# Attention and gated MLP in one program: the first token block takes its weights from the decoder, and the planner's costs and order are redone

## The chip, the cores and the metric

The program runs on one core of a Trainium2 chip. The metric is the device time of one execution in microseconds (us); less is better. The engines are PE (matrix products, with PEld for its weight loads), DVE (vector), ACT (activation functions, copies with a scale), POOL (elementwise work) and SP, which here only issues DMAs, in the order in which the program lists them.

## What is computed

Inputs are q, k, v of shape (4, 8, 1152, 64) in float32, and three weight matrices of a gated MLP in float64. Each batch's attention is computed for query rows that are averaged in pairs, so 576 query rows meet 1152 keys; the 8 heads' results stand side by side as rows of 512, and the MLP is applied to these 2304 rows.

```python
q_pool = q.reshape(B, H, S // 2, 2, D).mean(axis=3)
scores = (1 / sqrt(D)) * q_pool @ k.T
attn = softmax(scores)                     # float32, over 1152 keys
x = (attn @ v) as rows of H * D            # 2304 x 512
g = x @ w_gate                             # 512 x 1536
out = (g * sigmoid(g) * (x @ w_val)) @ w_out   # 1536 x 512
```

## The kernel before, in words

**Precision.** PE multiplies in a reduced float32 form (F32R). Each float32 operand is therefore split in a high part (a cast) and a low part (the rest), and a product is made of two or three matmuls.

**Attention.** The work is cut in 16 pairs of heads, `p`, each with nine tiles of 128 query rows; a *tile* below is one of these 144. A tile (`s_tile`) makes scores in three pieces of 384 keys: one in a PSUM bank `sb`, two in the double bank `sa` (PE, L499). DVE takes a running minimum of the first piece (L505) and then of the other two (L507, once per tile, so L507 counts tiles), ACT makes the exponentials `pn` (L515). A `unit` transposes three tiles' exponentials for 128 keys into a bank `pt` (PE, L557), ACT casts the high part `ph` (L562), DVE subtracts the low part `pl` (L565), PE multiplies both with `vs` into `po` (L573). `evac` adds the results up (L607, L610). POOL sums the denominators (L620, L621), DVE inverts them (L624), SP writes them to DRAM (`rs<-rc`, L632), reads them back spread over partitions (`rb<-rs`, L637), POOL multiplies (L644) and SP stores the result (`xd<-xf`, L646). For each pair q, k, v are loaded (L356 to L365), split on POOL, transposed on PE (L453) and copied to `kt`, `qt`, `qrt` by ACT or DVE (L458, L460).

**Weights.** The MLP's weights are 36 blocks of 512 KB: for each of 12 feature groups `f` a gate, a value and an output block. `decode_w(n)` turns a float64 block into the two float32 parts by integer work: SP loads the words `wraw` (L278, L280; two buffers), ACT takes the size (L286), DVE clamps, shifts, adds the low bits and the sign (L289, L293, L297, L301), ACT casts the high part into a buffer `ws` (L307), POOL subtracts the low part (L310), SP stores both to a DRAM block `wd` (L313). There is one `ws` buffer: the next block's cast waits until the store of this one has landed. The 36 decodes are placed from tile 27 to tile 70 (`DEC0`, `DEC1`).

**MLP.** Three blocks of 512 tokens run between the attention tiles from tile 39 on, the first 512 tokens (block 0) about from tile 39 to 75, blocks 1 and 2 each 36 tiles later; the last 768 tokens run as a `tail` with nothing beside them. For each `f`, `fetch` reads gate and value weights from `wd` into `wg` (3 buffers) and the output weight into `wo` (3 buffers) (L792); `hidden` makes the two first products (L801) in banks `pg`, the gate on ACT and DVE (L814 to L843), and the split `hh`, `hl` (L847, L851); `out_tile` multiplies with `wo` (L907) for three `f` at a time, and the results are added on DVE (L943). Before block 0 begins, the two `pg` banks are lent to the attention of the first batch (pairs 0 to 3): `other` gives every second `sb` and every third `pt` the name `pg`, and both uses take the two banks in turn.

**The order.** Every step is an `op` with a cost in us on its engine, a position in tiles, the steps that must precede it, the buffers that it takes and gives back, and `more`, the time from its end until its result is there (for a DMA, the landing). `Plan.order` builds a schedule from these costs, and the instructions of every engine are issued in that order; nothing is decided when the program runs, and each engine executes its list strictly in order. Where a step may run on one of several engines, the schedule picks one, or `KEPT` fixes it. `SHIFTS` is a table of two characters for each step that moves the step's position, by up to about five tiles; "PP" is zero. The planner's costs for DVE are lower than the trace's durations in many lines (0.468 us for L565, whose mean is 551 ns); the DMAs' `more` is between 1.6 and 3.5 us.

Of the kernel before, what the change touches and what calls it, by code (L numbers as in the profile page):

```python
# [20 lines left out]
def f32_of_bits(bits):  # L21
# [14 lines left out]
        "PPPPPPPiPPPPPPPPMSPPPPPPPPPPPPPPPPPPPPPPPPPPPPB8PPPPPPPPPPPPPPPPPPPPPPPPPPPPPPPPPPPPPPPPPPPPPPPPPPPPPPPP"  # L36
        "PPPPPPPPP\\PPPPPPPPPPPPPPPPPPPPPPPPPPPPPPP'PPPPPPPPPPPPPPPPPPPPPPPPPPPPPPPPQHPPPPPPPPPPPOPPPPPPPPPPPPPPNS"
        "PPPPPPPPPPPPPPPPPPPPPPPPPPPPPPPPPPPPR?PPPPPPPPPPS#PPPPPPPPPPPPLMPPPPPPPPPPPPOtPPPPPPPPPPPPPPPPPPPPPPPPPP"
        "PPPPPPPPPPPPPPPPPPPPPPQlPPPPPPPPPPPPPPPPPPPPPPPPPPPPPPPPPPPPPPPeT/PPPPPPPPPPPPPPPPPqPPPPPPPPPPPPPPPPPPPP"
        "PPPPPPPPPPPPPPPPPPPPPPPPPPL1PPTWPPPPPPPPPPPPPPPPPPPPPPPPPPPPPP"  # L40
    ),
    "pair": (
        "R%PPPPPPPPPPPPPPPPPPPPPPPPPPPPPPPPPPPPPPPPPPPPPPPPPPPPPPPPPPPPPPPPPPPPPPPPPPPPPPPPPPPPPPPPPPPPPPPPPPPPPP"
        "PPPPPPPPPPPPPPPPPPPPPPPPPPPPPPPPPPPPPPPPPPPPPPPrPPPPPPPPPPPPPPPPPPPPPPPPPPPPPPPPPPPPPPPCPPPPPPPPPPPPP0PP"
        "PPPPPPPPPPPPPPPPPPPPPPPPPPPPPPPPPPPPPPPPPPPPPPPPPPPPPPPPPPPPNnPPPPPPPPPPPPPPPPPiPPPPPPPPPPPPPPPPPPPPPPPP"
        "PPPPPPPPOOPPPPPPPPPPPPPPPPQ?PPPPPPPPPPPPPPPPPPPPPPPPPPPPPPQ?PPPPPPPPPPPPPPPPPPPPPPPPPPPPPPPPPPPPPPPPPPPP"
        "PPPPPPPPPPPPPPPPPPPPPPPPPPPPPPPPPPPP"
    ),
# [986 lines left out]
```

## Time and profile before

| | us |
|---|---|
| three runs | 1139.1, 1142.38, 1141.29 (median 1141.29) |
| the profiled execution | 1147.5, of which its span (first to last instruction) is 1145.7 |
| PE busy | 1031.4 (90% of the span) |
| DVE busy | 759.3 (66%) |
| ACT busy | 631.1 (55%) |
| POOL busy | 337.2 (29%) |
| mean granted PE clock | 0.954 |

In the profile, a row of the slices gives the busy share of 40 equal slices of the span in tenths; each slice is 28.6 us. A row of the waits reads: engine, the tile and line that waited, what released it, and us in total, times, longest. In a row of the timeline stand start, length, engine, line and operation, and in brackets the idle time ahead of it and who ended it. "SPq" is SP's issuing of a DMA.

### The profile page before, as it was taken

How to read it: one execution, taken by the hardware profiler on the slowest of the kernel's cores; microseconds unless marked ns; L12 is line 12 of the kernel's file. 1: busy time of each engine (PE TensorE's matmuls, PEld its weight loads, DVE VectorE, ACT ScalarE, POOL GpSimd, SP SyncE). 2: the span in 40 equal slices, each digit the busy share in tenths (PEclk: the TensorE clock that was granted, in tenths of full speed). 3: DMA queues.
4: the chain of work that ended last, by engine and by line, in shares of the span. 5: the costliest groups of instructions: out<-in, count | busy, mean ns of one | idle time of the engine just before them, and what ended most of it. 6: DMA issues, size and time to landing. Idle time of an engine off the chain costs nothing.

```text
span 1145.7 us, 17106 instructions
## 1 busy us (share of the span) xinstructions
PE 1031.4 (90%) x5937; PEld 918.2 (80%) x5937; DVE 759.3 (66%) x1427; ACT 631.1 (55%) x1471; POOL 337.2 (29%) x316
## 2 busy tenths in 40 slices
PE   5988877687878879999998999999999997899997
PEld 4878866576767767888997989889889986799996
DVE  5777777796878969868665767667676763422222
ACT  4776765476556655765664565657575753111112
POOL 5043142543526235252413232334141101200000
PEclk8999988788998989999998999999999998999999
DMA  4233366867697786565545464564443625634432
GB/s 154 63 82 77 61 197 176 262 232 161 225 209 229 251 186 207 161 204 176 146 107 136 153 119 154 119 202 115 125 117 94 113 88 90 225 116 127 140 114 74
DMA packets 94390, 171.46 MB, mean 150 GB/s; under 512 B 27424, under 2 KB 46752, under 8 KB 94304
## 3 DMA queue, kind: packets, MB, share of 16 engines
q1 hardware_dynamic: 94128, 169.98, 53.7%
q8 instruction: 47, 0.77, 0.3%
q14 instruction: 39, 0.32, 0.1%
q0 software_dynamic: 96, 0.26, 0.1%
q10 hardware_dynamic: 80, 0.13, 0.0%
HBM read 132.12 MB, written 28.39 MB: 140 GB/s over the span
## 4 chain that ended last, share of the span: by engine, by line
PE 67%; DMA 13%; DVE 10%; ACT 5%; issue 3%; SPq 1%; POOL 1%; DVEq 0%; POOLq 0%; ACTq 0%
PE pg L801 23%; PE po L573 10%; PE sa L499 8%; PE pt L557 8%; PE pg L907 6%; DMA wd<-ws 4%; PE sb L499 4%; DMA wg<-wd 3%; DMA rs<-rc 3%; PE pt L453 2%; ACT pn L515 2%; DVE junk L507 2%; DVE pl L565 2%; PE sa L907 1%; PE pt L907 1%
## 5 line engine op out<-in xcount | busy, mean ns | idle before, releaser
L801 PE MATMUL pg<-x,wg 128*128 128x512 f32 (+1 forms) x1152 | 320.4, 394 | 14.2 <-DMA wg<-wd 10.8
L565 DVE TENSOR_TENSOR pl<-pt,ph 128x384 fp32r<-128x384 f32 x396 | 213.1, 551 | 109.8 <-ACT ph L562 107.0
L562 ACT CAST ph<-pt 128x384 fp32r<-128x384 f32 x396 | 182.6, 483 | 141.4 <-PE pt L557 127.4
L801 PEld LDWEIGHTS pg<-x,wg 128*128 128x128 f32 x1152 | 206.1, 193 | 37.2 <-DMA wg<-wd 11.9
L557 PE MATMUL pt<-ident,pn 128*128 128x128 f32 x1056 | 188.4, 285 | 19.5 <-DVE pl L565 9.1
L573 PE MATMUL po<-ph,vs 128*128 128x384 f32 (+1 forms) x576 | 175.5, 318 | 1.7 <-DVE xs L610 1.7
L573 PE MATMUL po<-pl,vs 128*128 128x384 f32 (+1 forms) x576 | 172.2, 313 | 4.4 <-DVE pl L565 4.0
L507 DVE TENSOR_SCALAR_CACHE_REDUCE junk<-sa,mx 128x768 bf16<-128x768 f32 x144 | 145.8, 1012 | 42.4 <-PE sa L499 40.9
L557 PEld LDWEIGHTS pt<-ident,pn 128*128 128x128 f32 x1056 | 138.9, 147 | 38.8 <-issue 7.1
L515 ACT ACTIVATE pn<-sa,mx 128x768 f32<-128x768 f32 x144 | 130.9, 909 | 61.4 <-DVE junk L507 61.1
L499 PE MATMUL sa<-kt,qt 128*128 128x384 f32 x512 | 145.8, 371 | 6.9 <-ACT pn L515 6.8
L573 PEld LDWEIGHTS po<-pl,vs 128*128 128x128 f32 x576 | 111.7, 194 | 14.8 <-DVE pl L565 7.0
L573 PEld LDWEIGHTS po<-ph,vs 128*128 128x128 f32 x576 | 111.6, 194 | 11.1 <-DVE xs L610 1.7
L907 PE MATMUL pg<-wo,hh 128*128 128x512 f32 x288 | 114.7, 403 | 1.0 <-ACT hh L847 0.6
L499 PEld LDWEIGHTS sa<-kt,qt 128*128 128x128 f32 x512 | 91.5, 201 | 16.5 <-ACT pn L515 9.5
L851 POOL TENSOR_TENSOR hl<-ta,hh 128x512 fp32r<-128x512 f32 x36 | 47.2, 1310 | 161.9 <-ACT hh L847 141.8
L843 DVE TENSOR_TENSOR ta<-pg,ta 128x384 f32<-128x384 f32 x48 | 26.8, 558 | 94.8 <-ACT ta L839 67.6
L505 DVE TENSOR_REDUCE mx<-sb 128x1 f32<-128x384 f32 x128 | 70.6, 551 | 28.3 <-PE sb L499 27.1
L310 POOL TENSOR_TENSOR ws<-w,ws 128x512 fp32r<-128x512 f32 x36 | 49.3, 1368 | 121.3 <-ACT ws L307 107.0
L499 PE MATMUL sb<-kt,qt 128*128 128x384 f32 x224 | 65.3, 374 | 21.1 <-ACT pn L515 21.0
L847 ACT CAST hh<-ta 128x512 fp32r<-128x512 f32 (+1 forms) x60 | 34.7, 579 | 83.0 <-DVE ta L843 54.3
L515 ACT ACTIVATE pn<-sb,mx 128x384 f32<-128x384 f32 x128 | 75.8, 592 | 0.1
(116 smaller groups left out, 1635.2 us busy)
## 6 DMA issues: line engine op xcount, KB each, us to landing
wg<-wd SPq DMA_DIRECT2D x96, 512.0 KB
wo<-wd SPq DMA_DIRECT2D x48, 512.0 KB
wd<-ws SPq DMA_DIRECT2D x36, 512.0 KB
vraw<-in_v_dram SPq DMA_DIRECT2D x16, 576.0 KB
kraw<-in_k_dram SPq DMA_DIRECT2D x15, 576.0 KB
qraw<-in_q_dram SPq DMA_DIRECT2D x15, 512.0 KB
qt<-qt SPq DMA_DIRECT2D x60, 128.0 KB
wraw<-in_moe_w_gate_dram SPq DMA_DIRECT2D x12, 512.0 KB
```

Source lines behind the costliest of these rows:

```text
L310: nc.gpsimd.tensor_sub(cell["s"][:, 1], cell["w"], cell["s"][:, 0])
L499: nc.tensor.matmul(o[:, 0:KW], lhsT=lhsT, rhs=s[f"kt{jj}"][:, n * KW:(n + 1) * KW], start=(m == 0), stop=(m == len(terms) - 1))
L505: nc.vector.tensor_reduce(mx[:, 0:1], cell["b"][:, 0:KW], axis=AX.X, op=ALU.min)
L507: nc.vector.tensor_scalar(junk, cell["a"][:, :, 0:KW], mx[:, 0:1], None, op0=ALU.min, op1=ALU.min, accum_out=mx[:, 1:2])
L515: nc.scalar.activation(o[:, 0:2 * KW].rearrange("p (a k) -> p a k", a=2) if n == 0 else o[:, 2 * KW:S], cell["a"][:, :, 0:KW] if n == 0 el ...
L557: nc.tensor.transpose(cell["ps"][:, o:o + P], src, ident)
L562: nc.scalar.copy(cell["h"], cell["ps"][:, 0:GW])
L565: nc.vector.tensor_sub(cell["l"], cell["ps"][:, 0:GW], cell["h"])
L573: nc.tensor.matmul(o[:, c0:c1], lhsT=s["vs"][:, j, c, :], rhs=cell[x][:, c0:c1], start=(c == 0 and n == 0 and x == "h"), stop=(c == KC - 1 ...
L801: nc.tensor.matmul(o, lhsT=w[:, a, c * P:(c + 1) * P], rhs=x[c][b][:, 0:n], start=(c == 0 and m == 0), stop=(c == NC - 1 and m == 2))
L851: (nc.gpsimd if eng == "Pool" else nc.vector).tensor_sub(cell["l"][:, 0:n], cell["a"][:, 0:n], cell["h"][:, 0:n])
L907: nc.tensor.matmul(o, lhsT=cell[a][:, t * P:(t + 1) * P], rhs=w[:, b, :], start=(first and m == 0), stop=(last and m == 2),)
```

## The change

It touches the weights of block 0, the lent banks and the planner.

- **Block 0 uses decoded weights in place.** `decode` takes a `wg` or `wo` buffer instead of `ws` and leaves the two parts there; block 0's products read them from it. The store to `wd` stays, for blocks 1, 2 and the tail, but the cast no longer waits for the one before: it waits for a free `wg` or `wo` buffer, which is free when block 0's products and the store have both read it. Block 0's 36 fetches from `wd` are gone. `ws` is gone, and `wg` has four buffers instead of three.
- **The decodes move.** They are placed at block 0's own steps, five, four and one tiles ahead of the product (`DECODE`), instead of evenly from tile 27 to 70.
- **Banks.** `pg` becomes two names: `pg0` is lent to `sb`, `pg1` to `pt`, also for the first tiles of pair 4; in the MLP the gate product is always in `pg0` and the value product in `pg1`, output tiles alternate.
- **The planner** gets higher DMA costs, a new rule for the order in which takers of a buffer stand (`turn`: by the position of the step that begins the chain), and new tables `SHIFTS` and `KEPT`: most steps now have a shift, and some steps a fixed engine.

```diff
 SHIFTS = {
     "pair": (
-        "R%PPPPPPPPPPPPPPPPPPPPPPPPPPPPPPPPPPPPPPPPPPPPPPPPPPPPPPPPPPPPPPPPPPPPPPPPPPPPPPPPPPPPPPPPPPPPPPPPPPPPPP"
+        "lxIUO%I4<PN`TQK>_,=3=zUU@XX$PYWoPP0P>@q\\1OoZqP9KRP>YZOoP:O_[OPV\\;S/PYX3>CMvLkIVGWFcI_T7IGPwOrP_N`FvP'N7"
...
 KEPT = {
     "pair": (
-        "........."
+        "AAD.D.AA."
...
-    def op(self, cost, pos, fn, after=(), take=(), give=(), more=0.0, load=0):
+    def op(self, cost, pos, fn, after=(), take=(), give=(), more=0.0, load=0, turn=None):
...
         for name in take:
-            self.takers[name].append((pos, n))
+            self.takers[name].append((pos if turn is None else self.ops[turn][1], n))
...
         def hi():
-            cell["s"] = stage.tile([P, 2, 512], F32R, name="ws", tag="ws", bufs=decoding["ws"])
-            nc.scalar.copy(cell["s"][:, 0], cell["w"])
+            cell["w"] = new(("wg", "wg", "wo")[i], [P, 2, 512], F32R)
+            nc.scalar.copy(cell["w"][:, 0], cell["f"])
...
         def put():
-            nc.sync.dma_start(out=wd[n], in_=cell["s"].bitcast(F32))
+            nc.sync.dma_start(out=wd[n], in_=cell["w"].bitcast(F32))
...
-    decoding = {"wraw": 2, "wa": 1, "w32": 1, "ws": 1}
+    decoding = {"wraw": 2, "wa": 1, "w32": 1}
...
-            "wg": 3, "wo": 3, "hh": 3, "hl": 3, "ta": 2, "tb": 2, **{f"ob{t}": 1 for t in range(TB // P)},
+            "wg": 4, "wo": 3, "hh": 3, "hl": 3, "ta": 2, "tb": 2, **{f"ob{t}": 1 for t in range(TB // P)},
...
-        banks = {"sa": 1, "sb": 1, "pt": 2, "po": 1, "pg": 2}
+        banks = {"sa": 1, "sb": 1, "pt": 2, "po": 1, "pg0": 1, "pg1": 1}
...
-        def other(tag, p, turn):
+        def other(tag, p, turn, early):
-            return "pg" if p < HP and turn else tag
+            return {"sb": "pg0", "pt": "pg1"}[tag] if turn and (p < HP or p == HP and early) else tag
...
-            y = op({"SP": 1.7}, z + 8 - LEAD + 1.7, lambda p=p: spread(p, 0), after=[y], give=("rc",), more=2.1)
-            y = op({"SP": 1.3}, z + 8 - LEAD + 1.8, lambda p=p: spread(p, 1), after=[y], take=("rb",), more=2.1)
+            y = op({"SP": 1.7}, z + 8 - LEAD + 1.7, lambda p=p: spread(p, 0), after=[y], give=("rc",), more=10.0)
+            y = op({"SP": 1.3}, z + 8 - LEAD + 1.8, lambda p=p: spread(p, 1), after=[y], take=("rb",), more=4.0)
...
-        DEC0, DEC1 = 27.0, 70.0
-        for n in range(3 * NF):
-            plan.part("decode")
-            load, size, clamp, shift, low, sign, hi, lo, put = decode_w(n)
-            pos = DEC0 + (DEC1 - DEC0) * n / (3 * NF)
-            x = op({"SP": 1.46}, pos - 1.0, load, take=("wraw",), more=2.1, after=[at_tile(pos)])
+        def decode(n, tag, pos):
+            cell, load, size, clamp, shift, low, sign, hi, lo, put = decode_w(n)
+            x = f = op({"SP": 1.6}, pos - 1.0, load, take=("wraw",), after=[at_tile(pos - 1.0 + LEAD)], more=4.0)
...
-            x = op({"ACT": 0.53}, pos + 0.06, hi, after=[x], take=("ws",))
+            x = op({"ACT": 0.53}, pos + 0.06, hi, after=[x], take=(tag,), turn=f)
             x = op({"Pool": 1.5}, pos + 0.07, lo, after=[x], give=("w32",))
-            wput[n] = op({"SP": 0.8}, pos + 0.08, put, after=[x], more=3.0, give=("ws",))
+            wput[n] = op({"SP": 1.6}, pos + 0.5, put, after=[x], more=4.0)
+            return x, cell
...
-            return op({"SP": 0.8}, pos, load, after=[wput[n]], take=(tag,), more=3.5), cell
+            return op({"SP": 1.6}, pos, load, after=[wput[n]], take=(tag,), more=3.8), cell
...
         def block(blk, s0):
+            decoded = []
+            if blk == 0:
+                plan.part("decode")
+                for f in range(NF):
+                    at = s0 + 9.0 * (f // FG) + 2.0 * (f % FG)
+                    decoded.append([decode(3 * f + i, ("wg", "wg", "wo")[i], at + DECODE[i]) for i in range(3)])
...
-                    wg = [fetch(3 * f + i, "wg", pos - 3.0 + i) for i in range(2)]
-                    wo.append(fetch(3 * f + 2, "wo", pos + 1.0))
+                    if blk == 0:
+                        *wg, w = decoded[f]
+                        wo.append(w)
+                    else:
+                        wg = [fetch(3 * f + i, "wg", pos - 3.0 + i) for i in range(2)]
+                        wo.append(fetch(3 * f + 2, "wo", pos + 1.0))
...
+        DECODE = (-5.0, -4.0, -1.0)
```

How the instructions move. In the rows below, a row is one instruction of an engine in the order of its list: the line, the operation, the tile written and read, its shape, and a count where equal rows follow each other. The changed kernel's line numbers are 6 higher in these places.

First place: ACT in the middle of the decode, about tile 54, before. `wa` is the decoder's working tile, `ws` the decoded parts, `kt` the keys of the next pair, `ph` the high parts of the exponentials, `pn` the exponentials:

```order
L286 ACTIVATE wa<-wraw 128x512
L607 COPY tmp<-po 64x192
L562 CAST ph<-pt 128x384
L307 CAST ws<-w_3884 128x512
L458 ACTIVATE kt_3862<-pt 128x512
L562 CAST ph<-pt 128x384
L607 COPY tmp<-po 64x192
```

ACT with the change, where it copies the keys of the same pair:

```order
L313 CAST wo<-w_3739 128x512
L568 CAST ph<-pt 128x384
L292 ACTIVATE wa<-wraw 128x512
L464 ACTIVATE kt_3796<-pt 128x512
L568 CAST ph<-pt 128x384
```

The decoder's cast still stands a step or two ahead of the copy of the keys, but it writes a buffer of `wo` instead of the one `ws`.

Second place: SP around the eleventh and twelfth decoded block, before. `wd` is a DRAM block, `rs`, `rb`, `rc` the denominators' path:

```order
L313 DMA wd_87<-ws 128x1024
L278 DMA wraw<-in_moe_w_val_dram 128x4x128
L792 DMA wg<-wd_84 128x1024
L632 DMA rs_65<-rc 128x4x1 x2
L633 DMA rs_65<-rc 2x64x1
L313 DMA wd_88<-ws 128x1024
L280 DMA wraw<-in_moe_w_out_dram 128x512
L637 DMA rb<-rs_65 64x576 x2
L792 DMA wg<-wd_86 128x1024
```

SP with the change, at the store of the same two blocks:

```order
L319 DMA wd_86<-wg 128x1024
L366 DMA qraw<-in_q_dram 128x2x512
L371 DMA qraw<-in_q_dram 64x128 x2
L284 DMA wraw<-in_moe_w_val_dram 128x4x128
L319 DMA wd_87<-wg 128x1024
L652 DMA xd_58<-xf 128x576
```

The stores read `wg`, and no fetch `wg<-wd` stands between them.

Third place: SP where the last pair of heads ends, before. The `wg` rows fetch for block 2 and then for the tail:

```order
L633 DMA rs_76<-rc 2x64x1
L792 DMA wg<-wd_108 128x1024
L637 DMA rb<-rs_76 64x576 x2
L792 DMA wg<-wd_110 128x1024
L792 DMA wg<-wd_111 128x1024
L792 DMA wg<-wd_77 128x1024
```

SP with the change, at the same place:

```order
L639 DMA rs_76<-rc 2x64x1
L798 DMA wg<-wd_108 128x1024
L798 DMA wg<-wd_111 128x1024
L643 DMA rb<-rs_76 64x576 x2
L798 DMA wg<-wd_77 128x1024
L798 DMA wg<-wd_78 128x1024
```

Two fetches for block 2 now stand ahead of `rb<-rs`, which waits for `rs` to land; a third, `wd_110`, has moved further ahead, out of the rows shown.

More of the change, by code (lines that the diff above doesn't have):

```diff
@@ L529, in s_tile @@
             done["s", p, i] = a
-            x = op({"ACT": 0.88}, pos + EXP_AT, lambda: exp(0), after=[x], take=("pn", "sums") if i == 0 else ("pn",), give=("sa",))
+            x = op({"ACT": 0.88}, pos + EXP_AT, lambda: exp(0), after=[x], take=("pn", "sums") if i == 0 else ("pn",), give=("sa",), turn=f)
             done["p", p, i] = op({"ACT": 0.56}, pos + EXP_AT + 0.01, lambda: exp(1), after=[x], give=(sbank, "mx"))
@@ L578, in unit @@
             a = op({"PE": 0.33}, pos, tr, after=[done["p", p, i] for i, _ in tiles], take=(tbank,), load=-1)
-            b = op({"ACT": 0.37}, pos + HI_AT, hi, after=[a], take=("ph",))
+            b = op({"ACT": 0.37}, pos + HI_AT, hi, after=[a], take=("ph",), turn=a)
             x = op({"DVE": 0.468}, pos + LO_AT, lo, after=[b], give=(tbank,))
@@ L859, in hidden @@
                         {"PE": 3 * n * 0.000452}, pos + i * GV + c * GV / NC, lambda i=i, c=c: product(i, c),
-                        after=[x_done[key][c], wg[i][0], y, *([] if late is None else [at_tile(pos + i + LEAD - late)])],
-                        take=("pg",) if c == 0 else (), load=1, give=(give[i] if last else ()),
+                        after=[x_done[key][c], wg[i][0], y, *(put[i:i + 1] if last else ()), *([] if late is None else [at_tile(pos + i + LEAD - late)])],
+                        take=(f"pg{i}",) if c == 0 else (), load=1, give=(give[i] if last else ()),
                     )
@@ L890, in load @@
                 load_x(key, g0, n)
-            a = op({"SP": 2.4}, pos, load, after=[done["x", p] for p in pairs], take=take, more=2.5)
+            a = op({"SP": 3.2}, pos, load, after=[done["x", p] for p in pairs], take=take, more=4.0)
             cost = {"Pool": 0.3 + n * 0.0033, "DVE": 0.14 + n * 0.0016}
@@ L946, in out_tile @@
             for m in range(FG):
-                y = op({"PE": 0.69}, pos + 0.25 * m, lambda m=m: product(m), after=[hs[m][0], wo[m][0], y, at_tile(pos + LEAD - LATE)], take=("pg",) if m == 0 else (), load=1)
+                y = op({"PE": 0.69}, pos + 0.25 * m, lambda m=m: product(m), after=[hs[m][0], wo[m][0], y, at_tile(pos + LEAD - LATE)], take=(pg,) if m == 0 else (), load=1)
             if g == 0:
-                z = op({"ACT": 0.48, "DVE": 0.6}, pos + 0.8, put, after=[y], take=(f"ob{t}",), give=("pg",))
+                z = op({"ACT": 0.48, "DVE": 0.6}, pos + 0.8, put, after=[y], take=(f"ob{t}",), give=(pg,))
             else:
-                z = op({"DVE": 0.6}, pos + 0.8, put, after=[y, obs["w", t]], give=("pg",))
+                z = op({"DVE": 0.6}, pos + 0.8, put, after=[y, obs["w", t]], give=(pg,))
             obs["w", t] = z
```

199 lines of the change are left out of this document (103 added, 96 removed).

## The prediction

> **What bounds the kernel now.** First the page's slices, to see which engine is full where, and what the clock and the DMAs do meanwhile.
>
> ```profile
> PE   5988877687878879999998999999999997899997
> DVE  5777777796878969868665767667676763422222
> PEclk8999988788998989999998999999999998999999
> DMA  4233366867697786565545464564443625634432
> ```
>
> From the 16th slice on PE is full but for a dent at slice 34. Before that it is not, least of all in slices 5 to 15, where DVE and the DMAs are busiest. Next I counted the tiles by L507, which runs once per tile, in four windows, and asked for the engines' busy time in the same windows.
>
> ```profile
> L507 DVE TENSOR_SCALAR_CACHE_REDUCE junk<-sa,mx x24: 1006/1017/1020, 27.3 to 128.0; 128x768 bf16<-128x768 f32 x24
> L507 DVE TENSOR_SCALAR_CACHE_REDUCE junk<-sa,mx x12: 1002/1016/1019, 133.6 to 202.7; 128x768 bf16<-128x768 f32 x12
> L507 DVE TENSOR_SCALAR_CACHE_REDUCE junk<-sa,mx x37: 1000/1008/1019, 214.1 to 500.9; 128x768 bf16<-128x768 f32 x37
> 27.00:134.00 107.00, 96.13 (x652) 88.39 (x652) 80.51 (x167) 77.71 (x194) 31.18 (x33) 0.97 0.30 77
> 134.00:214.00 80.00, 56.41 (x318) 49.09 (x315) 58.69 (x116) 48.35 (x115) 28.78 (x27) 0.86 0.62 170
> 214.00:507.00 293.00, 251.19 (x1384) 217.64 (x1385) 240.37 (x425) 183.24 (x415) 124.93 (x103) 0.91 0.73 213
> 507.00:941.00 434.00, 426.29 (x2571) 381.73 (x2570) 303.50 (x584) 267.21 (x638) 124.65 (x121) 0.99 0.51 132
> 941.00:1000.00 59.00, 48.86 (x234) 40.72 (x233) 25.23 (x43) 17.48 (x35) 11.01 (x12) 0.94 0.61 156
> ```
>
> The windows' columns are window, length, busy PE, PEld, DVE, ACT, POOL, granted clock, DMA share, GB/s. I call the middle ones stages 1 to 4. Plain attention takes 107 / 24 = 4.46 us per tile. Stage 1 (tiles 28 to 39, decoding begins) takes 80 us for 12, which is 6.7 each. Stage 2 (tiles 40 to 76, decoding and block 0) takes 293 for 37. Stage 3 has the same MLP work per tile, from weights in DRAM, and PE is 426.29 / 434 = 0.98 busy: there is nothing to win but 7.7 us. PE's idle time is 23.6 us in stage 1, 41.8 in stage 2, 10.1 in stage 4. So the decoding is where the time lies, and the waits of stage 2 say why (the last row is of the whole span).
>
> ```profile
> ACT ws L307 <- DMA wd<-ws: 27.4, 7, 9.6
> PE pt L453 <- ACT kt L458: 16.2, 2, 9.0
> PE sb L499 <- ACT pn L515: 12.7, 5, 7.0
> ACT ws L307 <- DMA wd<-ws: 36.8, 11, 9.6
> ```
>
> One such wait in the timeline, SP's, ACT's and PE's rows:
>
> ```profile
> 330.48 2.18 SPq L313 DMA_DIRECT2D wd<-ws  x1
> 344.21 0.62 ACT L307 CAST ws<-w 128x512 fp32r<-128x512 f32 x1 [9.62 <-DMA wd<-ws]
> 344.74 0.59 ACT L458 ACTIVATE kt<-pt 128x512 fp32r<-128x512 f32 x1
> 345.38 0.37 PE L453 MATMUL pt<-identr,ks 128*128 128x128 f32 x1 [8.98 <-ACT kt L458]
> ```
>
> The cast of a decoded block needs the one `ws`, whose store was issued 13.7 us earlier. ACT stands still for 9.62 us, the copy of the next keys stands behind the cast, and PE waits 8.98 us for that copy. DVE and POOL stop too.
>
> **Stage 1.** Of the 36 decodes, these rows of L289 put 8 in stage 1 and 28 in stage 2.
>
> ```profile
> L289 DVE TENSOR_SCALAR wa<-wa x8: 408/422/1098, 149.4 to 211.3; 128x512 f32<-128x512 f32 x8
> L289 DVE TENSOR_SCALAR wa<-wa x28: 406/424/1483, 220.4 to 471.7; 128x512 f32<-128x512 f32 x28
> L289 DVE TENSOR_SCALAR wa<-wa 128x512 f32<-128x512 f32 x36 | 20.5, 568 | 2.1 <-ACT wa L286 1.8
> L293 DVE TENSOR_SCALAR wa<-wa 128x512 int32<-128x512 int32 x36 | 24.6, 683 | 0.4
> L297 DVE SCALAR_TENSOR_TENSOR wa<-wraw,wa 128x512 int32<-128x512 int32 x36 | 35.5, 987 | 0.3
> L301 DVE SCALAR_TENSOR_TENSOR w<-wraw,wa 128x512 int32<-128x512 int32 x36 | 32.0, 890 | 6.0 <-POOL ws L310 5.4
> ```
>
> In DVE's list of the changed kernel one decode stands ahead of the 40th tile, 35 behind. Stage 1 becomes plain attention: 12 x 4.46 = 53.5, and one decode on DVE, 0.568 + 0.683 + 0.987 + 0.890 = 3.13 us: 57 in all, a gain of **23**. It cannot be much more, as PE has 96.13 / 2 = 48 us of work in 12 such tiles. It is 17 if ACT again stands 6.6 us at the first raw block:
>
> ```profile
> ACT wa L286 <- DMA wraw<-in_moe_w_gate_dram: 9.6, 2, 6.6
> ```
>
> **Stage 2.** *Gone:* the waits for the store, 27.4 us, with PE's 16.2 + 12.7 = 28.9 behind ACT; I take 27.4 off the path. 293 - 27.4 = 265.6. *Added:* 35 - 28 = 7 decodes, 7 x 3.13 = 21.9 us on DVE, which then has 240.4 + 21.9 = 262.3 us of work. That does not fit unseen in 265.6. Its share today is 240.4 / 293 = 0.82; 0.98 is what the planner reaches for PE in stage 3. I take 0.93, nearer to the upper end, since the stops that kept DVE idle are those that go: 262.3 / 0.93 = 282, a gain of **11**. Bounds: 0.98 gives 268 (gain 25), 0.88 gives 298 (loss 5).
>
> The 36 fetches for block 0 (18.9 of the 293 x 0.213 = 62 MB that stage 2 moved) cost PE nothing by themselves; without them the remaining transfers have more room. I count no gain for that, nor for a better clock than 0.91. What the change puts in the way: the cast now waits for a `wg` or `wo` buffer, with the exponentials and casts of attention queued behind it on ACT, and PE behind those. With four `wg` the buffer's last reader stands a tile or more earlier in PE's list, and its store several tiles earlier, so I take nothing; if that cover fails it costs at most what the old wait did, 27.4. And block 0's products wait for POOL's low part itself, with attention's matmuls behind them on PE. In the changed lists most casts stand two to five tiles ahead of their first product, a few only one. The nearest row of PE waiting for weights is below: 3.6 us each, so four of them would cost 14. I take nothing, as a decoded part is there without a landing.
>
> ```profile
> PE pg L801 <- DMA wg<-wd: 10.8, 3, 5.7
> ```
>
> The skill has a price for a store that speaks against this term. The Trainium skill, "DMA: Bandwidth & Descriptors", section "Anatomy of one DMA", fits about 2.0 us plus bytes / 436e3 (for DMAs issued from GpSimd): an estimate of 3.2 us for 512 KB. By that the store would have landed before ACT came to the cast, the 27.4 would be nothing to win, and the sum would end at 1125 instead of 1098. The trace shows 13.7 us from issue to cast, and decides.
>
> **Stage 3 and 4: fetches ahead of a blocked queue.** At the end of a pair SP waits for `rs` to land, and fetches stand behind it.
>
> ```profile
> 943.15 0.55 SPq L633 DMA_DIRECT2D rs<-rc  x1
> 943.84 3.51 SPq L792 DMA_DIRECT2D wg<-wd  x1
> 955.63 1.12 SPq L637 DMA_DIRECT2D rb<-rs  x2
> 956.84 15.17 SPq L792 DMA_DIRECT2D wg<-wd  x4
> 959.99 1.65 PE L801 MATMUL pg<-x,wg 128*128 128x512 f32 x3 [5.74 <-DMA wg<-wd]
> PE pg L801 <- DMA wg<-wd: 5.0, 2, 4.8
> ```
>
> PE ran dry for 5.74 us here, and for 5.0 in stage 3 (last row). The planner's 2.1 us for this landing becomes 10.0, and in the new SP list two fetches of block 2 stand ahead of `rb<-rs` here, a third earlier still. I take **5.5** in stage 4 and **4** in stage 3; both could be nothing. All of stage 3 is in a new order, though: it can gain at most its 7.7 us of idle time, and lose about as much (+8) where new orders meet real durations.
>
> **Start and banks.** Up to 134 us the bank names and the order change. Before stage 1 PE idles 107 - 96.1 = 10.9 us; two uses that share two banks in turn wait for each other, and no longer do. Between a gain of 5 and a loss of 4 I take 0. In the MLP gate and value alternated anyway: 0. The tail behind 1000 us is PE's own work: 0.
>
> **Sum.** -23 - 11 - 4 - 5.5 = -43.5. The profiled execution took 1147.5 (span 1145.7); it lies 6.2 above the median of the runs, 1141.3. 1147.5 - 43.5 = 1104, and on the runs' scale **1098 us**.
>
> **Rivals.** All on the runs' scale.
>
> *DVE stays the limit (faster, by less).* For it: 35 decodes in 37 tiles, and planner costs for DVE that are too low. The spread of one operation, alone and beside POOL:
>
> ```profile
> L297 DVE SCALAR_TENSOR_TENSOR wa<-wraw,wa x36: 675/692/1816, 150.7 to 474.7; 128x512 int32<-128x512 int32 x36
> L310 POOL TENSOR_TENSOR ws<-w,ws 128x512 fp32r<-128x512 f32 x36 | 49.3, 1368 | 121.3 <-ACT ws L307 107.0 <-DVE wa L289 9.3 <-DVE pl L565 5.1
> ```
>
> A decode's four operations average 0.782 us, while half of L297's 36 took under 0.692 and the longest 1.816. If the excess over about 0.54 grows with POOL's share, (124.9 + 7 x 1.37) / 282 = 0.48 against 0.43, DVE gets 140 x 0.24 x 0.11 = 3.7 us more, 266. At a share of 0.88 stage 2 takes 302, and the time is 1118; at today's 0.82 it takes 324, and the time is 1140, no change. The Trainium skill, "GPSIMD Engine Reference", section "Key points", says that GpSimd shares its SBUF interfaces with VectorE and contends with instructions of two SBUF inputs; by that rule the time would be 1118 rather than 1098. L297 has two such inputs, and its longest agree. Against the low shares: ACT's stops, which emptied DVE, are gone. Chances 0.14 and 0.04.
>
> *The stop comes back as a wait for a buffer.* 282 + 27.4 = 309 in stage 2: 1125. Against it speaks the buffers' distance. Chance 0.03.
>
> *The decode's own loop sets the pace (no change, or slower).* Two raw buffers: a load waits for the sign step of the block before last, then lands, then five steps on ACT and DVE. Today:
>
> ```profile
> L307 ACT CAST ws<-w x36: 602/621/647, 155.8 to 478.1; 128x512 fp32r<-128x512 f32 x36
> 134.19 12.97 DMA wraw<-in_moe_w_gate_dram
> ```
>
> (478.1 - 155.8) / 35 = 9.2 us per block. Today block 0 is fed ahead of time; with the change its products cannot outrun the loop, and PE carries attention behind them. If the first cast comes at 134 + 57 = 191 and each next 9.2 later, the last comes at 513, beside the 76th tile: stage 2 takes 322, and the sum is -23 + 29 - 9.5 = -3.5: 1138, no change. With 12.97 to land, 0.68 + 3.13 of steps and each step behind one attention step of about 0.8, two blocks take 20 us, 10 each: the last cast at 541, stage 2 takes 350, and the time is 1166, **slower**. It decides from 9.3 us per block on. Against it: ACT waited for a raw block only twice (9.6 above), against 36.8 for stores, so the loop was held by the store. Chances 0.03 and 0.06.
>
> *Better than forecast.* DVE at 0.98 in stage 2 (gain 25) and the start's 5: 1079. Chance 0.14.
>
> **Numbers.** The forecast has 0.56. A measurement of this kernel can tell about 0.3% (3.4 us) from no change. Faster by more: 0.56 + 0.14 + 0.14 + 0.03 = 0.87; within: 0.04 + 0.03 = 0.07; slower: 0.06. The range reaches from 1068 (all gains at their ends: 25 + 25 + 5 + 7.7 + 5.7 + 5 = 73) to 1130, past the weaker gains of 1118 and 1125; 0.13 lies beyond.
>
> **What would show it.** Right: no row of ACT's cast behind a store; tiles 28 to 39 in about 57 us; tiles 40 to 76 in about 282 with DVE near 0.93 busy; PE's wait for `wg<-wd` near zero. DVE as limit shows as PE waiting for `pl` and `kt` of DVE with DVE full. The loop shows as ACT's L292 waiting for `wraw`, or PE's L807 for POOL. The buffer shows as ACT's L313 waiting for PE or the store. The prediction is wrong if stage 2 stays above 305 us, or if stage 3 takes 10 us more than 434.

## The result, and the profile after

| | before | after |
|---|---|---|
| median of the runs, us | 1140.19 (4 runs, 1136.03 to 1142.38) | 1088.71 (4 runs, 1087.85 to 1089.76) |
| ratio | | 0.9553, 95% interval 0.9523 to 0.9583 |
| profiled execution, us | 1147.5, span 1145.7 | 1088.12, span 1086.3 |
| PE busy, mean granted clock | 1031.4 (90%), 0.954 | 1011.2 (93%), 0.986 |
| bytes moved by DMA | 171.46 MB | 152.57 MB |

The change makes the kernel 4.5% faster. The page's slices of after (27.2 us each):

```profile
PE   6999996889789989899999999999989999999997
DVE  6878886999879898977566776777666664422222
PEclk9999997999989999999999999999999999999999
DMA  4233226686556762765375635674534647534342
```

PE has 9 from the second slice to the sixth, where before had 7 to 9, and the dent at slice 34 is gone. From the seventh to the seventeenth several slices still stand at 6 to 8. I counted tiles in after by L513 (before: L507) and cut its span at the same tiles as before's; the tail begins at its first activation on ACT.

| tiles | before, us | predicted | after, us | gain | predicted gain |
|---|---|---|---|---|---|
| start and tiles 1 to 27 | 133.6 | 133.6 | 121.4 | 12.2 | 0 |
| 28 to 39 (stage 1) | 80.5 | 57 | 55.1 | 25.4 | 23 |
| 40 to 76 (stage 2) | 293.1 | 282 | 281.7 | 11.4 | 11 |
| 77 to 143 (stage 3) | 431.6 | 430 | 429.7 | 1.9 | 4 |
| to the tail (stage 4) | 50.8 | 45 | 41.6 | 9.2 | 5.5 |
| tail | 156.3 | 156.3 | 156.8 | -0.5 | 0 |

The gains add up to 59.6 us, while the medians fell by 51.5: the profiled execution of before lies 7.3 us above its median, and that of after 0.6 below. Some 8 us of these gains belong to that one execution of before; experiment 6 shows where part of them may lie.

The windows of after in the same columns as in the prediction (length, PE, PEld, DVE, ACT, POOL, clock, DMA share, GB/s), for stages 1, 2 and 3:

```profile
121.00:176.00 55.00, 45.46 (x305) 40.30 (x304) 41.17 (x89) 38.40 (x96) 19.93 (x20) 0.93 0.37 87
176.00:458.00 282.00, 246.59 (x1389) 207.43 (x1388) 254.98 (x442) 192.14 (x437) 133.08 (x111) 0.97 0.63 183
458.00:888.00 430.00, 425.12 (x2558) 376.79 (x2558) 292.99 (x566) 275.16 (x652) 126.62 (x120) 1.00 0.54 136
```

DVE's share in stage 2 is 254.98 / 282 = 0.90. The waits of after: the first row is of stage 1, the next three of stage 2, the last two of the whole span.

```profile
PE pg L505 <- ACT pn L521: 5.8, 1, 5.8
PE pt L563 <- DVE pl L571: 9.5, 12, 2.0
PE pt L563 <- ACT kt L464: 8.8, 2, 8.2
ACT wg L313 <- DVE w L307: 12.9, 10, 2.9
ACT wa L292 <- DMA wraw<-in_moe_w_gate_dram: 14.9, 2, 8.0
PE pg L807 <- DMA wg<-wd: 5.2, 3, 3.2
```

No cast waits behind a store or for a buffer. What is left of the stops stands in the fifth row: ACT waits twice for a raw block of the gate, and PE behind it (5.8 in the first row, 8.2 in the third). The decoder's casts:

```profile
L313 ACT CAST wg<-w x24: 602/620/637, 174.6 to 442.0; 128x512 fp32r<-128x512 f32 x24
L313 ACT CAST wo<-w x12: 613/622/677, 194.7 to 456.8; 128x512 fp32r<-128x512 f32 x12
```

The loop takes (456.8 - 174.6) / 35 = 8.06 us per block, against 9.21 before.

### The profile page after: what moved, and what is told of

It reads as the page before. It is cut to its first block, busy times and chain, and to the rows that moved or that the text cites. A ratio compares the mean times of both kernels' runs of the same rounds, so it can differ in the third digit from the quotient of the medians.

```text
span 1086.3 us, 17069 instructions
## 1 busy us (share of the span) xinstructions
PE 1011.2 (93%) x5937; PEld 891.1 (82%) x5937; DVE 747.8 (69%) x1403; ACT 638.2 (59%) x1489; POOL 341.0 (31%) x322
## 2 busy tenths in 40 slices
DMA packets 89205, 152.57 MB, mean 140 GB/s; under 512 B 26848, under 2 KB 46176, under 8 KB 89120
## 4 chain that ended last, share of the span: by engine, by line
PE 64%; DVE 16%; DMA 8%; ACT 7%; issue 4%; POOL 0%; SPq 0%; POOLq 0%; DVEq 0%; ACTq 0%
PE pg L807 21%; PE po L579 10%; PE sa L505 8%; PE pt L563 7%; PE pg L913 7%; PE sb L505 4%; DVE junk L513 3%; DMA wg<-wd 3%; DMA wraw<-in_moe_w_gate_dram 3%; DVE pl L571 3%; ACT pn L521 2%; DVE wa L303 2%; PE pt L459 2%; DVE w L307 2%; PE pt L913 2%
## 5 line engine op out<-in xcount | busy, mean ns | idle before, releaser
L807 PE MATMUL pg<-x,wg 128*128 128x512 f32 (+1 forms) x1152 | 307.8, 388 | 10.5 <-DMA wg<-wd 5.2
L571 DVE TENSOR_TENSOR pl<-pt,ph 128x384 fp32r<-128x384 f32 x393 | 211.8, 551 | 74.9 <-ACT ph L568 72.4
L563 PE MATMUL pt<-ident,pn 128*128 128x128 f32 x1047 | 184.4, 277 | 21.1 <-DVE pl L571 11.7
L579 PE MATMUL po<-ph,vs 128*128 128x384 f32 (+1 forms) x576 | 178.8, 324 | 3.0 <-DVE xs L616 1.9
L513 DVE TENSOR_SCALAR_CACHE_REDUCE junk<-sa,mx 128x768 bf16<-128x768 f32 x144 | 145.7, 1012 | 35.1 <-PE sa L505 32.4
L563 PEld LDWEIGHTS pt<-ident,pn 128*128 128x128 f32 x1047 | 130.6, 141 | 47.1 <-DVE pl L571 15.4
L505 PE MATMUL sa<-kt,qt 128*128 128x384 f32 x512 | 139.2, 361 | 4.2 <-ACT pn L521 4.2
L579 PEld LDWEIGHTS po<-ph,vs 128*128 128x128 f32 x576 | 109.9, 191 | 11.4 <-DVE xs L616 4.4
L505 PEld LDWEIGHTS sa<-kt,qt 128*128 128x128 f32 x512 | 88.6, 194 | 13.0 <-ACT pn L521 6.9
L398 POOL TENSOR_SCALAR ks<-kraw 128x576 fp32r<-128x576 f32 (+2 forms) x32 | 22.3, 698 | 141.6 <-PE pt L459 140.9
L505 PE MATMUL sb<-kt,qt 128*128 128x384 f32 x220 | 61.5, 361 | 1.9 <-ACT pn L521 1.1
```

The lines of the kernel that those rows point to most:

```text
L505: nc.tensor.matmul(o[:, 0:KW], lhsT=lhsT, rhs=s[f"kt{jj}"][:, n * KW:(n + 1) * KW], start=(m == 0), stop=(m == len(terms) - 1))
L513: nc.vector.tensor_scalar(junk, cell["a"][:, :, 0:KW], mx[:, 0:1], None, op0=ALU.min, op1=ALU.min, accum_out=mx[:, 1:2])
L563: nc.tensor.transpose(cell["ps"][:, o:o + P], src, ident)
L571: nc.vector.tensor_sub(cell["l"], cell["ps"][:, 0:GW], cell["h"])
L579: nc.tensor.matmul(o[:, c0:c1], lhsT=s["vs"][:, j, c, :], rhs=cell[x][:, c0:c1], start=(c == 0 and n == 0 and x == "h"), stop=(c == KC - 1 ...
L807: nc.tensor.matmul(o, lhsT=w[:, a, c * P:(c + 1) * P], rhs=x[c][b][:, 0:n], start=(c == 0 and m == 0), stop=(c == NC - 1 and m == 2))
```

## The experiments

**The theory:** the time comes from the decodes leaving stage 1, from the store's stop going (stage 2), and from fetches that the planner's longer `rs` landing puts ahead of the blocked queue (stages 3 and 4). **Rivals:** the tables alone do it; the bank change does it; DVE's work holds the rest; the stop only moves on, to the raw loads; the decode loop sets the pace. A ratio below is to the kernel before as it ran beside the experiment (medians 1139.0 to 1141.2).

**1. The store alone.** The kernel before with two real `ws` buffers, in the old order.

```diff
-            cell["s"] = stage.tile([P, 2, 512], F32R, name="ws", tag="ws", bufs=decoding["ws"])
+            cell["s"] = stage.tile([P, 2, 512], F32R, name="ws", tag="ws", bufs=2)
```

> The kernel before with a second real ws buffer; every engine's list is word for word that of before, so only the cast's wait for the last store is gone. If the store's stops were on the path, ACT's 36.8 us behind stores vanish and the program gains 25 to 35 us (about 1110). If DVE was the real limit of the decode, or if the stop only moves on to the next landing, it gains under 10 us.

1121.96 us, ratio 0.9852 (0.9804 to 0.99). The waits of its ACT for raw blocks:

```profile
ACT wa L286 <- DMA wraw<-in_moe_w_gate_dram: 11.1, 2, 6.3
ACT wa L286 <- DMA wraw<-in_moe_w_val_dram: 9.6, 3, 4.3
ACT wa L286 <- DMA wraw<-in_moe_w_out_dram: 4.9, 2, 4.0
```

The cast no longer waits for a store, and stages 1 and 2 are 25.8 us shorter (75.0 and 272.8). But ACT now waits 25.6 us for raw blocks, 9.6 before. So the store's stop was real, and part of it moves on to the loads; the gain of 18.3 us lies between the two that were expected. Stage 1 gains only 5.5 of its 25.4 us by this; the rest comes with the decodes leaving it, though no run moves the decodes alone.

**2. DVE's work.** After without the operation that adds the lowest three bits of each weight's fraction (L303, 36 times 0.92 us): this part of the decode is left out.

> The changed kernel without L303 (the low three bits of each weight are left out), lists otherwise the same: DVE loses 36 x 0.924 = 33 us. If DVE carries tiles 40 to 76, the program gains 20 us or more there (about 1068). If what is left there are stops of ACT and chains of waits between the engines, it gains under 8 us.

1076.74 us, 0.9468 (0.9409 to 0.9528), 12 less than after. 33 us of DVE work are gone and stage 2 shrinks by 16 (281.7 to 265.7): by this, DVE is on the path for about half of the time there. The size is rough, since the profiled execution is the longest of the four runs (1072.68 to 1085.55), and its start and its stage 3 are 4.2 and 7.3 us longer than after's.

**3. A third raw buffer.** After with `bufs=3` for `wraw`, in the same order.

> The changed kernel with a third real buffer for raw words, lists the same: SP need not wait for the sign step before it issues a load. If ACT's three stops behind raw words (14.9 + 2.1 us, with PE 5.8 and 8.2 us behind them) come from late issue, they go and the program gains 8 to 14 us (about 1077). If the loads are late because the transfers themselves take that long, under 3 us.

1092.14 us, 0.959 (0.9542 to 0.9638): no gain.

```profile
ACT wa L292 <- DMA wraw<-in_moe_w_gate_dram: 14.8, 2, 7.8
```

The waits stay as they were (14.9 in after). So these loads do not wait for a buffer; they are issued late or land late.

**4. The tables.** After with every entry of `SHIFTS` zero and every entry of `KEPT` free, so that the structure and the planner's costs stand alone.

> The changed kernel with all shifts at zero and no fixed engine: the weights in place, the banks and the DMA costs alone, ordered by the planner's rule. If the removed stops and the later decode are the gain, tiles 28 to 39 stay near 55 us and the program stays 20 us or more under the kernel before (1110 to 1120). If the tables make the gain, it is no faster than before (1140 or more).

1104.28 us, 0.9698 (0.9658 to 0.9738). Of the 51.5 us the structure and costs bring 35.9, the tables 15.6. The start and tiles 1 to 27 take 134.1 us, as before; stage 1 takes 59.3, so that 21.2 of its 25.4 us need no table; stage 3 takes 423.7, less than after's 429.7; PE never waits for `wg<-wd`.

**5. The planner's `rs` landing.** The same, with `more` for `rs` and `rb` put back to 2.1 and 2.1.

> The changed kernel with zero tables (1104.3 us), and in the planner the landing of rs and rb back at 2.1 us each. If the planner's knowledge of that landing is what keeps PE from waiting for wg fetches, waits of PE for wg come back, 5 to 12 us of them from tile 77 on, and the program takes 1109 to 1117. If the fourth wg buffer is what does it, PE still has no such wait and the time stays within 3 us of 1104.

1106.14 us, 0.9699 (0.9659 to 0.9739): the same, and again no wait for `wg`. The longer planned landing is not what removed these waits. It does shorten SP's own waits for `rs` (103.0 us with 2.1, 18.2 with 10.0), but here that moves the time by no more than 2 us.

**6. The banks.** The kernel before with `pg0` and `pg1` as in the change (cut to the core).

```diff
-            return "pg" if p < HP and turn else tag
+            return {"sb": "pg0", "pt": "pg1"}[tag] if p < HP and turn else tag
...
-                    cell[i] = bank("pg", [P, 512])
+                    cell[i] = bank(f"pg{i}", [P, 512])
```

> The kernel before with the bank change alone (pg0 lent to the scores, pg1 to the transposes, pg0 and pg1 in the MLP; not for pair 4), everything else as before. If the start's 12 us came from the banks, tiles 1 to 27 take about 109 us instead of 117.8 and the program gains 8 us or more. If they came from the tables, tiles 1 to 27 stay within 2 us of 117.8 and the program within 5 us of before.

1136.3 us, 0.9984 (0.9955 to 1.0013): no difference, and tiles 1 to 27 take 119.7 us. Its stage 2 in the window's columns, and the store's stop in it:

```profile
219.20:499.20 280.00, 244.33 (x1384) 209.20 (x1383) 238.08 (x422) 181.76 (x414) 122.74 (x102) 0.95 0.76 219
ACT ws L307 <- DMA wd<-ws: 25.1, 8, 7.5
```

A kernel as fast as before has a stage 2 of 280 us here, with 25.1 us of the stop in it and a granted clock of 0.95; the profile of before had 293, 27.4 and 0.91. So one profile's stage 2 is uncertain by about as much as the 11.4 us that the table gives as its gain.

**7. Later raw loads planned for.** After with the load's `more` at 12.0 instead of 4.0, so that the order expects late landings.

> The changed kernel with the raw words' landing planned as 12 us instead of 4, near the 12.8 us of the chain; the order of the decode moves with it. If ACT's stops behind raw words are what is left, ACT's 14.9 us behind the first loads and PE's 5.8 + 8.2 us behind ACT go: 1076 to 1082. If a table tuned for 4 us loses as much in its new order, within 3 us of 1088.7.

1123.79 us, 0.986 (0.9829 to 0.9891), 35 more than after. Its casts, and its engines in a window from the 40th tile on:

```profile
L313 ACT CAST wg<-w x24: 611/620/631, 181.3 to 512.6; 128x512 fp32r<-128x512 f32 x24
L313 ACT CAST wo<-w x12: 607/619/643, 207.8 to 536.2; 128x512 fp32r<-128x512 f32 x12
169.00:434.00 265.00, 223.90 (x1272) 188.35 (x1271) 213.93 (x398) 175.08 (x402) 111.39 (x99) 0.96 0.55 159
```

Neither expected outcome came. ACT never waits for a raw block now, and stages 1 and 2 are the shortest so far (47.0 and 264.9). But the loop is planned at (536.2 - 181.3) / 35 = 10.1 us per block. In stage 2 PE does 1272 matmuls where after does 1389, and the rest of block 0 stands in stage 3, which takes 488.4 instead of 429.7. This is the loop that is too slow, the rival that the prediction gave 0.06; here the planner's order makes it so.

**8. The tables of the second half.** After with its tables up to the ninth pair (`p` of 8) and block 0, and zero behind (cut to the core).

```diff
-            plan.part(*(("first",), ("pair", "lone"), ("pair",), ("pair", "last"))[(p > 0) + (p >= HP) + (p == NP - 1)])
+            plan.part(*(("first",), ("pair", "lone"), ("pair",), ("late",))[(p > 0) + (p >= HP) + (p >= 9)])
...
-            plan.part("mlp", f"mlp{blk}")
+            plan.part(*(("mlp", "mlp0") if blk == 0 else ("late",)))
```

> The changed kernel with its tables up to the eighth pair and block 0, and zero shifts and no fixed engines from the ninth pair, block 1 and the tail on. With zero tables everywhere the stretch from tile 77 to 144 took 423.7 us against 429.7, and the step to the tail 40.3 against 41.6. If the late tables cost that time, it is 1081 to 1084. If the earlier order feeds into the later one, so that the stretches can't be added up, within 3 us of 1088.7.

1082.14 us, 0.9497 (0.9463 to 0.9531), 6.6 less than after. Stage 3 takes 425.0: the late part of the tables costs time. Tiles 1 to 27 keep their gain (110.3 us), so that gain is of the early part.

**9. The fourth `wg` buffer.** The kernel before with `"wg": 4`, for the planner as well.

> The kernel before with four wg buffers instead of three, for the planner too. If the fourth buffer is what lets the fetches run ahead of SP's wait for rs, PE's 10.8 us behind wg go and the stretch from tile 144 to the tail shrinks from 50.8 to about 42: 1128 to 1132. If it is the rest of the change, PE's waits for wg stay above 8 us and the time within 4 us of 1140.

1121.27 us, 0.9825 (0.9799 to 0.9851). Its slices:

```profile
PE   5988967697888878999999999999999999999997
```

The dent at slice 34 is gone and PE never waits for `wg<-wd`. Stage 3 falls from 431.6 to 422.9, stage 4 from 50.8 to 42.2. This one number is worth more than the prediction's steps for stages 3 and 4 together, and more than was expected of it.

**10. Why the stores and loads were late.** In before, the store whose landing cost ACT 9.62 us (shown in the prediction) stands right behind the writes of `rs` in SP's rows of the timeline:

```profile
328.85 0.92 SPq L632 DMA_DIRECT2D rs<-rc  x2
329.82 0.56 SPq L633 DMA_DIRECT2D rs<-rc  x1
330.48 2.18 SPq L313 DMA_DIRECT2D wd<-ws  x1
```

The store behind the stop of 8.2 us stands in the same place and took 11.2 us to land. These two stops are 17.8 of ACT's 36.8 us behind stores. Two more, of 6.9 and 5.2 us, are of another kind: the store lands in 4.1 and 5.2 us, but it is issued late, because in SP's list it stands behind `rb<-rs`, which waits until `rs` has landed. SP's rows for the first of them, then ACT's:

```profile
406.26 0.56 SPq L633 DMA_DIRECT2D rs<-rc  x1
417.66 1.14 SPq L637 DMA_DIRECT2D rb<-rs  x2
418.89 0.53 SPq L313 DMA_DIRECT2D wd<-ws  x1
423.11 0.62 ACT L307 CAST ws<-w 128x512 fp32r<-128x512 f32 x1 [6.92 <-DMA wd<-ws]
```

POOL had this block ready at 410.9, 8.0 us before the store was issued (6.7 us for the other). So `rs` stops ACT in two ways, by stores that land late beside it and by stores that SP issues late behind it. The remaining 6.9 us are short waits for stores without either.

In after the raw load that stopped ACT in stage 1 stands right behind the writes of `rs` too; SP's rows, then ACT's:

```profile
156.54 0.55 SPq L639 DMA_DIRECT2D rs<-rc  x1
157.13 0.46 SPq L284 DMA_DIRECT2D wraw<-in_moe_w_gate_dram  x1
170.00 0.66 ACT L292 ACTIVATE wa<-wraw 128x512 f32<-128x512 f32 x1 [6.91 <-DMA wraw<-in_moe_w_gate_dram]
```

It took 12.87 us from issue to use, and ACT stood still for 6.91 of them. `rs<-rc` writes 1152 separate pieces of 4 bytes. Two theories for the late landing: the order of the queue (transfers behind `rs` in SP's queue wait for it), or the pieces themselves (they slow whatever is in flight). First the queue: the kernel before with `rs` issued by POOL.

```diff
-                    nc.sync.dma_start(out=rs[p][j, 0:QT * P].rearrange("(t p) -> p t", p=P), in_=s["rc"][:, t0:t0 + QT])
-                nc.sync.dma_start(out=rs[p][:, QT * P:SP], in_=s["rc"][:, QT:QT + 1])
+                    nc.gpsimd.dma_start(out=rs[p][j, 0:QT * P].rearrange("(t p) -> p t", p=P), in_=s["rc"][:, t0:t0 + QT])
+                nc.gpsimd.dma_start(out=rs[p][:, QT * P:SP], in_=s["rc"][:, QT:QT + 1])
```

> The kernel before, with the three small DMAs rs<-rc of each pair issued by POOL instead of SP, everything else in the same order. In the trace of before, a 512 KB DMA issued on SP right behind rs<-rc lands after 10 to 16 us, others mostly after 3 to 6. If the small packets ahead of it in SP's queue are what delays it, ACT's long waits behind stores (9.6, 8.2, 6.9) and PE's waits for wg go, and the program gains 15 to 30 us (1110 to 1125). If the small packets slow everything on the DMA engines whichever queue they are in, or if POOL loses as much by issuing them, it stays within 5 us of 1140.

1163.83 us, 1.0208 (1.0171 to 1.0244): slower, which neither theory expected. Its six runs lie between 1150.75 and 1170.21, and the profile is of the shortest. SP's wait for `rs` in before, then, of this kernel, the same wait, two others, and the landing of L632's and of L633's transfers:

```profile
SPq L637 <- DMA rs<-rc: 121.2, 20, 9.6
SPq L637 <- DMA rs<-rc: 206.3, 20, 19.1
ACT ws L307 <- DMA wd<-ws: 32.3, 10, 9.6
PE sb L499 <- DMA qrt<-qrt: 19.2, 5, 7.1
DMA to landing us min/median/max: 7.9/9.1/10.1
DMA to landing us min/median/max: 9.3/14.1/18.1
```

ACT waits for stores almost as long as before (32.3 us against 36.8), but mostly in the second way: 20.0 of the 32.3 us stand behind three stores that SP issued late, because it now waits 206.3 us for `rs`. One store landed late beside `rs` (9.6 us, which cost ACT 5.4). So these waits don't separate the two theories; the landings counted in experiment 11 do: there, large transfers on SP's queue are late beside an `rs` of POOL as well. Then the same in the kernel of experiment 8:

> The changed kernel with the late tables zero (1082.1 us), and rs<-rc issued by POOL. If the small packets ahead in SP's queue delay the raw words, ACT's waits of 6.9 and 8.0 us behind them go and the program gains 8 to 14 us (1068 to 1074). If the queue is not the reason, within 3 us of 1082.

1076.66 us, 0.9432 (0.9406 to 0.9457), 5.5 less than experiment 8, between the two that were expected. Here the raw loads no longer stand behind the `rs` writes in SP's list, where SP stood 5.7 us waiting for DVE: the load of stage 1 is issued at 149.9 us instead of 158.6. ACT's waits for raw blocks fall from 15.3 us to 3.1, and stages 1 and 2 from 334.4 to 320.6, but stage 3 loses 7. So the list's order has a part in the stops, through the time of issue.

**11. Without small pieces.** The kernel of experiment 8, where DVE transposes the inverted denominators so that SP writes them as 36 pieces of 128 bytes (cut to the writes; the transpose and the reads, four DMAs instead of two, are left out here).

```diff
-                for j in range(2):
-                    t0 = j * (QT + 1)
-                    nc.sync.dma_start(out=rs[p][j, 0:QT * P].rearrange("(t p) -> p t", p=P), in_=s["rc"][:, t0:t0 + QT])
-                nc.sync.dma_start(out=rs[p][:, QT * P:SP], in_=s["rc"][:, QT:QT + 1])
+                for b in range(4):
+                    nc.sync.dma_start(out=rs[p][:, b * 32:(b + 1) * 32], in_=s["rt"][b * 32:b * 32 + NTILE, :])
```

> The changed kernel with the late tables zero (1082.1 us), where rs is written in rows: DVE transposes the denominators in 32 x 32 blocks and SP stores 4 x 9 pieces of 128 bytes instead of 1152 of 4 bytes; SP reads them with four DMAs instead of two. The planner's order is the same. In before, after and both kernels with rs on POOL, no 512 KB DMA took over 8.5 us unless rs was in flight, and about half took over 9 when it was. If the 4-byte pieces are the cause, rs lands in 3 us instead of 10, no 512 KB DMA takes over 9 us, ACT's waits of 8.0 and 6.9 us behind raw words go, and the program takes 1066 to 1074. If something else at the end of a pair is the cause, the long landings stay and the time is within 4 us of 1082.

1062.12 us, 0.9319 (0.9282 to 0.9355): the fastest of all, 20 less than experiment 8 and 27 less than after. The same place of the timeline, SP's and ACT's rows, then stage 2's window:

```profile
156.17 1.37 SPq L642 DMA_DIRECT2D rs<-rt  x4
157.58 0.39 SPq L284 DMA_DIRECT2D wraw<-in_moe_w_gate_dram  x1
163.45 0.71 ACT L292 ACTIVATE wa<-wraw 128x512 f32<-128x512 f32 x1
169.00:438.00 269.00, 243.72 (x1388) 204.05 (x1386) 252.84 (x445) 191.47 (x437) 133.34 (x115) 0.99 0.58 191
```

The load is issued at the same time behind `rs`, and ACT starts on it 6.5 us earlier without a wait. Nowhere does ACT wait for a raw block. DVE reaches 252.84 / 269 = 0.94. Stages 1 and 2 take 317.4 us, against 334.4 in experiment 8. SP no longer waits for `rs` either (15.8 us in experiment 8); how much of the 20 us comes from that, and how much from the landings, was not separated. I counted in the traces, for each 512 KB transfer, the time from issue to its last landing event, apart by whether an `rs` write was in flight:

| kernel | with `rs` in flight: count, median, longest, over 9 us | without |
|---|---|---|
| before | 29, 11.2, 16.1, 19 | 187, 4.2, 8.5, 0 |
| after | 37, 9.6, 14.2, 23 | 143, 3.7, 8.1, 0 |
| before, `rs` issued by POOL | 27, 8.9, 13.1, 13 | 189, 4.3, 7.9, 0 |
| experiment 8 | 34, 9.7, 14.5, 20 | 146, 3.9, 8.3, 0 |
| experiment 8, `rs` issued by POOL | 34, 9.1, 14.7, 17 | 146, 3.9, 7.6, 0 |
| `rs` in pieces of 128 bytes | 18, 3.6, 7.0, 0 | 162, 3.8, 6.3, 0 |

In these kernels no 512 KB transfer took over 9 us without the small pieces beside it, from either queue, and with larger pieces none did at all. (In experiment 1's kernel four of 185 without `rs` took 9.2 to 9.9; they were issued within 5 us of one another.) That settles the cause of the late landings.

## Why the prediction was right, and where it was not

The time fell inside the range, and the mechanism of the two largest terms was the one named: decodes that leave stage 1, and a store that no longer stops ACT. On the runs' scale the gain is 51.5 us where the sum has 43.5. By the steps:

- **Stage 1 (23 us): right, the size in part by luck.** 55.1 us against 57, gain 25.4. The bound in the text, ACT standing 6.6 us at the first raw block, did come true (6.91); by the prediction's own working that leaves a gain of 17. Plain attention made up for it: tiles 1 to 27 fell from 117.8 to 108.9 us, and at that pace 12 tiles take 48.4 us where the sum has 53.5. Without the stop stage 1 takes 47.5 (experiment 11).
- **Stage 2 (11 us): right in size, by two errors that cancel, and by a size that is itself uncertain.** DVE's work was put at 262.3 us and measured 255.0. The sum added 28 instructions to before's 425; there are 442, 11 fewer, at 254.98 / 442 = 0.58 us each 6.3 us. ACT has 437 - 415 = 22 more, where two for each of seven decodes make 14: some of the work that DVE shares with ACT has gone there. I had taken the choice of engines as fixed. The share was put at 0.93 and measured 0.90. Experiment 11 reaches 0.94, with the order of experiment 8 (279.6 us for stage 2) and without ACT's waits for raw blocks. The 293.1 us of before come from one profile, and experiment 6 had 280.1 with the stop still in it. The granted clock rose from 0.91 to 0.97, for which the prediction took nothing; what that is worth was not separated.
- **The store's stop: right as the near cause, not the root.** Experiment 1 shows it real, and 16 of its 36.8 us moving on to the raw loads. The root of most of it was the `rs` write: two stores landed late beside it (17.8 us of the stop), and two were issued late behind SP's wait for it (12.1). The prediction read "13.7 us from issue to cast" as the price of a 512 KB store and set the 3.2 us that it worked out from the Trainium skill's "DMA: Bandwidth & Descriptors", section "Anatomy of one DMA", aside. The traces show both: a median of 4.2 us without `rs` in flight, 11.2 with it. The page's rule was near for the ordinary transfer, and what followed from it here (no stop to win) was wrong, since the stores that stopped ACT longest landed late or were issued late; in the stop of 6.92 us ACT came to the cast 2.7 us before the store was even issued.
- **Start and banks (0): the missed term, 12.2 us.** This is most of the distance between the sum of 43.5 and the 59.4 by which the span fell. The prediction looked at the banks, and these bring nothing there (experiment 6). The early part of the tables did it (experiments 4 and 8). PE's waits up to tile 27, of before, then of after:

```profile
PE sa L499 <- ACT pn L515: 5.9, 6, 1.8
PE sb L499 <- DMA qrt<-qrt: 4.7, 2, 2.9
PE pt L453 <- DVE qhl L398: 2.8, 1, 2.8
```

```profile
PE sa L505 <- ACT pn L521: 2.0, 4, 0.9
PE pt L459 <- DVE identr L329: 6.6, 1, 6.6
```

Before, PE waited 5.9 us for exponentials, 4.7 for a copy of the queries, 2.8 for a split on DVE; after, 2.0 for the exponentials, and the other two are gone. These rows stood in the trace of before. A bound of 5 us was too tight where the idle time alone was 10.9, and the 16 us ahead of the first tile, of which 3.3 went, were not looked at. The granted clock rose there too (0.93 to 1.00 from 16 to 121 us), but experiments 8 and 11 show 0.95 and keep the gain.

- **Stages 3 and 4 (4 + 5.5): right in sum, wrong in mechanism.** The step "the planner's 2.1 us for this landing becomes 10.0" falls: with 2.1 put back no wait returns (experiment 5). The fourth `wg` buffer removes the waits by itself, with the tables and DMA costs of before (experiment 9). The prediction listed that buffer and gave it no price. Stage 3 could have gained 8.7, and the late tables gave most of it back (experiments 4 and 8).
- **DVE as the limit (0.14): partly there.** Experiment 2 finds it on the path for about half of stage 2. One reason for it was wrong, that the planner's costs for DVE are too low:

```profile
327.01 0.54 DVE L571 TENSOR_TENSOR pl<-pt,ph 128x384 fp32r<-128x384 f32 x1
327.48 0.67 DVE L960 TENSOR_TENSOR ob<-pg,ob 128x512 f32<-128x512 f32 x1
```

The next instruction starts 0.47 us after this one of 0.54: durations overlap, and the planner's 0.468 is the distance from start to start. Over the 283 times in after that an instruction follows one of L571 without idle time, the median distance is 0.469 us.

- **The other rivals.** No cast waited for a `wg` or `wo` buffer. The loop's pace came out at 8.06 us per block, under the 9.3 from which it would have decided. This is also just stage 2's length over its 35 decodes, so it doesn't tell by itself what sets the pace; that a third raw buffer gains nothing (experiment 3) speaks against the loop. Experiment 7 shows what it costs at 10.1: 35 us rather than the 68 between 1098 and 1166. The late products stand in stage 3, which grows by 58.7 us while stages 1 and 2 shrink by 24.9.

## What to carry to other kernels

When a large transfer is late, first see whether it was issued late or landed late, and what was issued just ahead of it, before giving it a deeper buffer: here a few kilobytes in pieces of 4 bytes delayed large transfers in flight and held up the list behind them, and one small transpose on DVE was worth 20 us where a third raw buffer was worth nothing. Compare a stage's length with that of a second kernel of equal time before trusting a gain of some ten us in it. Price each number that a change touches, a buffer count included, and each stage's waits, the start included, even where the change seems to aim elsewhere. A table of shifts can win in one half of a kernel and lose in the other, so it is worth trying by halves.

## What was unexpected in the hardware

The three DMAs that write 1152 pieces of 4 bytes took 8 to 18 us each to land where POOL issued them, and of the 512 KB transfers beside such writes about half to two thirds took over 9 us (13 of 27 to 19 of 29), whichever engine issued the small ones. Written as 36 pieces of 128 bytes, they left none over 7.0 us. Which part of the transfer path the small pieces hold was not tried and stays open.
